# Where the words of a float64 weight are shifted and masked, in PSUM or in SBUF, in a convolution and mixing kernel on one core

## The chip, the cores and the metric

One NeuronCore of one Trainium2 chip runs the whole program. The metric is the device time of one execution in microseconds (us); lower is better. Times inside a profiled execution are counted from the start of its span.

## The reference

`x` is 8 x 4224 x 192 in float32. A softmax over seven taps weights a causal convolution along the sequence, and a low-rank mix along the sequence and a two-layer perceptron follow:

```python
w = np.exp(weight_gen - max); w = w / (sum(w) + 1e-09)       # over the 7 taps, 8 heads
out = np.einsum('bshk,bskhg->bshg', w, x_unf)                # the convolution: y
h = xt @ U @ V                                               # U: 4224 x 32, V: 32 x 4224
u = x + h.transpose(0, 2, 1)
ch = np.maximum(u @ w_ch1, 0.0) @ w_ch2                      # 192 -> 768 -> 192
return (u + ch).astype(np.float32)
```

`U`, `V`, `w_ch1` and `w_ch2` come in as float64. The kernel reads them as pairs of 32-bit words.

## The kernel before, in words

There are 88 blocks of 384 rows (11 for each of the 8 batches). A block `i` goes through the convolution (`p`: one tap's product; `acc`: their sum in PSUM; `y`), the projection `zp` of `y` on `U`, the mix `d` or `u` with `V` and the result of the projection, and the perceptron (`h`, `gh`, `gl`, `ab`, `o`). The mix needs the projection of a whole batch. So the program has a first stage, which makes the convolution of batch 0 (blocks 0 to 10) and prepares the weights, and a steady part, in which the perceptron of one block runs beside the convolution of the next batch.

**Splitting the weights.** A float64 is split into two or three fp32r parts, since TensorE multiplies in fp32r. `f64_split` (line 188) does this for a piece of up to 128 x 396 numbers, in steps that the rest of this text calls `P<part>.<step>`. There are twelve parts: 0, 1, 6 are pieces of `U`; 2, 3, 4 of `V`; 5, 8, 9 of `w_ch1`; 7, 10, 11 of `w_ch2`. Part numbers follow the loads, not quite the work: part 9 is split before part 8, and part 11 before part 10. The steps before:

- step 0, ScalarE: the high word, scaled, into the PSUM bank `pt_..._t` (Prelu with a scale);
- step 1, ScalarE: the low word into the PSUM bank `pt_..._x`;
- step 2, VectorE: the word in bank `t`, in place, shifted left by 3;
- step 3, ScalarE: bank `t` rounded to fp32r is the top part (`hi`, or straight into `ucat`, `w1h`, `w2c`);
- step 4, VectorE: bank `t` masked to its sign and exponent is `s`;
- step 5, VectorE: the low word times `s` is the low part (`lf`);
- step 6, TensorE: a matmul with minus the identity takes the top part off bank `t` (and for `w_ch1` and `w_ch2` another adds the low part);
- step 7, ScalarE: what is left in bank `t` is the rest (`r` for `V` and for part 9, otherwise straight into `ucat`, `w1l`, `w2c`).

Bank `t` is the one PSUM buffer of its pool. `hi`, `lf`, `s` and `r` are SBUF tiles of tags of their own, two buffers each.

**The three pieces of `V`.** `v_stores` (line 342) stores the parts of a piece to DRAM by three DMAs: `C<part>.0` the top, `C<part>.1` the rest (`vt<-v_r` in the profile), `C<part>.2` the low part. `v_load` (line 360) fetches a quarter of them by four DMAs into the one buffer `vq`, and `v_place` (line 368) copies that quarter into `vcat` on ScalarE. There are four such rounds, `L0 V0` to `L3 V3`; a load waits for the copy before it.

**What sets the order.** Every instruction is issued through a helper (line 30, `L30` in the profile) that keeps the program order on its engine. All DMAs are issued by SyncE, one after the other. In the first stage the order is a hand-written string, `FIRST` (line 1026), of codes: `P` steps of the split, `U` the load of a part, `C`, `L`, `V` as above, `M` products (`p` on GpSimd; `v` on VectorE, which reads the softmax weights from a copy `wq` in PSUM, code `Q`), `A` sums, `F` and `Y` first and last of a sum, `S` steps of a softmax, `x` and `D` loads of `x`, `W` loads of `weight_gen`, `Z` the projection. The line with the buffers is

```python
tiles[what] = first.tile([P, CHV], dt, tag=what, name=f"{name}_{what}", bufs=2)[:, :n]
```

Of the kernel before, what the change touches and what calls it, by code (L numbers as in the profile page):

```python
# [10 lines left out]
F32 = mybir.dt.float32  # L11
F32R = mybir.dt.float32r
I32 = mybir.dt.int32
U32 = mybir.dt.uint32
AF = mybir.ActivationFunctionType
# [29 lines left out]
def conv_moe_kernel(  # L45
# [17 lines left out]
    nc = Pinned(tc)  # L63
# [5 lines left out]
    P = 128  # L69
# [5 lines left out]
    D2 = D - P  # L75
# [106 lines left out]
    CH, CHV = 384, 396  # L182
# [5 lines left out]
    def f64_split(name, raw, n, hi, shaped, lo=None, rest=None, after=None):  # L188

        tiles = {}

        def tmp(what, dt=F32):
            if what not in tiles:
                tiles[what] = first.tile(
                    [P, CHV], dt, tag=what, name=f"{name}_{what}", bufs=2,
                )[:, :n]
            return tiles[what]  # L200

        def bank(what):
            if what not in tiles:
                pool, tag = (ps_d, "d") if what == "t" else (ps_first, "px")
                tiles[what] = pool.tile([P, 512], F32, tag=tag, name=f"pt_{name}_{what}")[:, :n]
            return tiles[what]

        low, high = raw[:, :n, 0], raw[:, :n, 1]

        def top():  # L210
            return shaped(tmp("hi", F32R)) if hi is None else hi

        def rem():
            return shaped(tmp("r")) if lo is None else lo

        def low_word():
            return rest if rest not in (None, True) else shaped(tmp("lf", F32R))

        def ti():
            return bank("t").bitcast(I32)  # L220

        def onto_t(terms):

            for m, term in terms:
                nc.tensor.matmul(
                    shaped(bank("t")), signs[m], term,
                    start=False, stop=True, skip_group_check=True,
                )


        steps = [
            lambda: nc.scalar.activation(
                bank("t"), high.bitcast(F32), AF.Prelu, scale=2.0**-112,
                alpha=-(2.0**32),
            ),
            lambda: nc.scalar.copy(bank("x"), low.bitcast(U32)),
            lambda: nc.vector.tensor_scalar(
                ti(), ti(), 3, None, op0=ALU.logical_shift_left
            ),
            lambda: nc.scalar.copy(top(), shaped(bank("t"))),  # L240
            lambda: nc.vector.tensor_scalar(
                tmp("s", I32), ti(), -(2**23), None, op0=ALU.bitwise_and
            ),
            lambda: nc.vector.scalar_tensor_tensor(
                low_word(), shaped(bank("x")), 2.0**-52,
                shaped(tmp("s", I32).bitcast(F32)), op0=ALU.mult, op1=ALU.mult,
            ),
            lambda: onto_t([(1, top())] + ([(0, low_word())] if rest is None else [])),
            lambda: nc.scalar.copy(rem(), shaped(bank("t"))),
        ]  # L250
        if after is None:
            return steps, []
        return steps, after(top, rem, low_word)
# [8 lines left out]
    def prep_u():  # L262
        n = CH // R
        src = words(u_in.rearrange("(p j) r -> p j r", p=P))
        for j0 in range(0, NJ, n):
            m = min(n, NJ - j0)
            raw = stage(f"u{j0}")
            nc.sync.dma_start(
                raw[:, : m * R].rearrange("p (j r) w -> p j (r w)", r=R),
                src[:, j0 : j0 + m],  # L270
            )
            yield f64_split(
                f"u{j0}", raw, m * R, ucat[:, j0 : j0 + m, :R],
                lambda a: a.rearrange("p (j r) -> p j r", r=R),
                ucat[:, j0 : j0 + m, R : 2 * R], ucat[:, j0 : j0 + m, 2 * R :],
            )

    def prep_w1():
        for c0 in range(0, DF, CH):
            cs = slice(c0, c0 + CH)  # L280
            ws = slice(2 * c0, 2 * (c0 + CH))
            raw = stage(f"w1a{c0}")
            nc.sync.dma_start(
                raw[:, :CH].rearrange("p n w -> p (n w)"), words(w1_in[:P])[:, ws]
            )
            yield f64_split(f"w1a{c0}", raw, CH, w1h[:, cs], flat, w1l[:, cs])

        raw = stage("w1b")
        for i in range(2):
            nc.sync.dma_start(  # L290
                raw[i * D2 : (i + 1) * D2, :CH].rearrange("p n w -> p (n w)"),
                words(w1_in[P:])[:, 2 * i * CH : 2 * (i + 1) * CH],
            )
        yield f64_split("w1b", raw, CH, None, flat, after=w1_copies)
# [684 lines left out]
    def soften(n):  # L979
# [35 lines left out]
    M1 = [0.262, -0.107, 0.14, -0.282, -0.017, -0.391]  # L1015
    M2 = [-0.081, -0.032, 1.559, 0.826, 0.748, 0.146]
# [8 lines left out]
    F_KIND = [0, 0, 1, 1, 1, 2, 0, 3, 2, 2, 3, 3]  # L1025
    FIRST = """
        I S0 x0 S0 R S0 S0 S0 S0 W1 S0 S1 U0 x1 P0.0 P0.1 M0.3p S1 P0.2 U1 S1 S1 P0.4 Q0 S1 x2
        S1 M0.2p P0.3 P0.6 U2 M0.0d P0.5 F0.2t P0.7 M0.4v P1.0 P1.2 S1 P1.4 A0.3t M1.0p P1.1
        A0.4t Q1 M0.6v M0.5v P1.3 P1.6 P1.5 A0.0t P1.7 M1.5d A0.6t Q2 P2.0 P2.2 M2.0v M1.1d W2
        M1.3v P2.3 A0.1v P2.1 F1.0t M2.2p U3 P2.4 S2 A1.2t P2.6 P2.7 Y0.5 P3.0 F2.0a A1.5t A1.1t  # L1030
        S2 M1.4v P2.5 Q3 P3.2 A2.2v D0 S2 S2 M2.5d P3.3 P3.1 x3 A1.6t P3.4 C2.1 M2.1v Z0 U4
        M2.3v M3.3p A1.3t C2.0 M3.2v P3.5 P3.6 M3.0d P3.7 U5 A1.4t P4.0 P4.2 A2.1t S2 A2.6t
        A2.3t S2 M2.4v P4.4 C2.2 Y1 P4.1 M3.4v F3.2a P4.3 A2.5t A3.3v P4.6 M3.6p S2 A3.0t Q5
        P4.7 P5.0 P4.5 M3.5v U6 M4.0d A2.4t x4 M5.0v C3.2 P5.1 P5.2 C3.1 M4.4d Z1 C3.0 W3 Q4
        M4.2v Y2 Q6 A3.1t P5.4 F4.2a P5.5 A3.6t A3.5t P5.3 P5.6 A4.0v P6.1 Z2 A4.4v S3 Y3.4
        M5.4d P5.7 P6.0 C4.1 C4.0 M4.3v F5.0a M5.2p C4.2 M5.1v M4.6v S3 A4.1t A4.3t A4.6t D1
        A5.1v P6.2 S3 A5.4v S3 P6.3 A4.5t Y4 D2 S3 M6.0v D3 P6.6 A5.2t M6.2d M5.3v P6.7 A5.5t S3
        L0 M6.5d F6.0a A6.3t S3 U7 P6.4 Z3 P6.5 M5.6v P7.0 M6.1p A6.6t P7.1 Q8 A6.2t Q7 P7.2
        P7.4 U8 A5.6v M6.4v P7.5 P7.3 V0 M8.0p P7.6 P7.7 Z4 U9 Y5.3 M7.2d P9.0 M7.0v D4 M7.5d
        A6.1t M7.1v M7.4v A6.5t P9.2 L1 A6.4t D5 F7.0a Q9 P9.1 Z5 D6 Y6 A7.4v P9.4 A7.1v F8.0a  # L1040
        M8.3v W4 M8.5d A7.2t M8.4p M8.1p M8.2v V1 P9.3 P9.5 Z6 A8.3v S4 A7.3t P9.6 A8.4v S4 Q10
        M9.0v C9.0 M9.2p M9.1p P9.7 P8.1 P8.0 A7.6v S4 M10.0p A8.1t A8.2t P8.2 P8.3 Y7.5 L2
        F9.0a U10 U11 P8.4 A8.6t M9.4v P8.5 V2 Z7 P8.6 P8.7 C9.2 A9.1t Y8.5 M9.3v M10.1d A9.2t
        P11.0 C9.1 M9.5v M10.3d S4 M9.6p A9.5t A9.3t P11.2 L3 D7 F10.0a A10.2t P11.1 P11.4 S4
        P11.5 P11.3 V3 S4 A10.1v P11.6 A9.6v A10.4v Z8 S4 Q11 T1 P11.7 A9.4t M10.5p P10.0 M10.6v
        A10.3t M11.2p A10.5t P10.2 M11.3v Y9 Y10.6 P10.3 P10.4 P10.1 D8 Z9 P10.5 M11.0d B1
        F11.2a M11.6p Z10 e0 P10.6 C9.3 d0 M11.4p D9 M11.5p A11.0v e1 A11.1v e2 d1 e3 e6 e4
        A11.3v e7 e5 A11.4t e8 D10 P10.7 D11 A11.5v Y11.6
    """
    with (  # L1050
        tc.tile_pool(name="first", bufs=2) as first,
# [165 lines left out]
```

## Time and profile before

| | |
|---|---|
| three runs | 1076.41, 1077.33, 1078.96 us; median 1077.33 us |
| the profiled execution's own time | 1078.56 us |
| its span, first to last instruction | 1076.8 us |
| TensorE matmul busy | 1062.4 us, 99% |
| VectorE, ScalarE, GpSimd busy | 912.1 us (85%), 803.1 us (75%), 843.6 us (78%) |
| mean granted TensorE clock | 0.998 of full speed |

The profiled execution took 1.23 us more than the median of the three, and 1.76 us of its time lie outside its span. Busy shares are means over two stages that differ: the first 80 us, where the weights are split, and the rest.

### The profile page before, as it was taken

What the parts mean: (1) busy time and instruction counts of PE and PEld (TensorE: products, weight loads), DVE (VectorE), ACT (ScalarE), POOL (GpSimd) and SP (SyncE); (2) the same over time, 40 slices, a digit from 0 to 9 for tenths busy, and PEclk for the clock granted to TensorE, in tenths of its full rate; (3) what the DMA queues carried; (4) which work ended last, traced back from release to release, by engine and by line L of the source; (5) the groups of instructions that cost most, each with busy time, mean ns of one, the idle gap of its engine ahead of it and who ended that gap; (6) DMA issues with size and microseconds to landing.
All of it is one profiled execution on the core that took longest, in us unless ns stands there. A gap on an engine that the chain in (4) does not pass through costs nothing.

```text
span 1076.8 us, 20185 instructions
## 1 busy us (share of the span) xinstructions
PE 1062.4 (99%) x6631; PEld 1040.8 (97%) x6631; DVE 912.1 (85%) x1704; ACT 803.1 (75%) x1934; POOL 843.6 (78%) x474
## 2 busy tenths in 40 slices
PE   7989999999999999999999999999999999999998
PEld 6768999999999999999999999999999999999998
DVE  7989899898889899898998998898998988755553
ACT  4678788877778777777777777777778777676664
POOL 8999899898988999898997999899998989400000
PEclk9999999999999999999999999999999999999999
DMA  7863444453443534444444444344443432323331
GB/s 224 238 179 98 138 120 129 119 161 102 131 134 99 156 112 123 143 118 129 133 111 130 140 116 137 111 134 135 109 144 110 118 99 83 102 75 95 90 96 48
DMA packets 132760, 133.66 MB, mean 124 GB/s; under 512 B 80696, under 2 KB 106552, under 8 KB 132528
## 3 DMA queue, kind: packets, MB, share of 16 engines
q1 hardware_dynamic: 132656, 132.38, 43.1%
q8 instruction: 52, 0.85, 0.3%
q14 instruction: 52, 0.43, 0.1%
HBM read 79.10 MB, written 53.23 MB: 123 GB/s over the span
## 4 chain that ended last, share of the span: by engine, by line
PE 92%; DMA 2%; ACT 2%; DVE 1%; POOL 1%; issue 1%; SPq 1%; ACTq 0%; POOLq 0%; DVEq 0%
PE h L30 43%; PE ab L30 42%; PE zp L30 4%; PE u L30 2%; DMA vq<-vt 1%; ACT vcat L30 1%; POOL p L30 1%; DMA w<-in_moe_w_ch_dram 1%; SPq L30 1%; DMA x<-in_x_dram 0%; DVE p L30 0%; PE d L30 0%; PE acc L30 0%; POOL wr L30 0%; PE zr L30 0%
## 5 line engine op out<-in xcount | busy, mean ns | idle before, releaser
L30 POOL TENSOR_TENSOR p<-x,wr 128x576 f32<-128x576 f32 (+1 forms) x340 | 661.3, 1965 | 70.9 <-DVE acc L30 62.6
L30 PE MATMUL ab<-w2c,gh 128*128 128x384 f32 x1584 | 482.4, 354 | 0.1
L30 ACT ACTIVATE gh<-h 128x384 fp32r<-128x384 f32 x528 | 257.5, 492 | 155.6 <-PE h L30 153.6
L30 PE MATMUL ab<-w2c,gl 128*128 128x192 f32 x1584 | 371.8, 254 | 0.0
L30 DVE SCALAR_TENSOR_TENSOR gl<-h,gh 128x384 fp32r<-128x384 f32 x528 | 282.7, 551 | 82.6 <-ACT gh L30 80.6
L30 DVE TENSOR_TENSOR acc<-acc,p 128x576 f32<-128x576 f32 x400 | 299.6, 750 | 0.4
L30 PEld LDWEIGHTS ab<-w2c,gl 128*128 128x128 f32 x1584 | 297.8, 190 | 0.0
L30 PEld LDWEIGHTS ab<-w2c,gh 128*128 128x128 f32 x1584 | 292.2, 188 | 0.6 <-ACT ab L30 0.6
L30 PE MATMUL h<-hi,w1h 128*128 128x384 f32 x528 | 182.1, 345 | 0.8 <-DVE lo L30 0.4
L30 PE MATMUL h<-lo,w1s 128*128 128x384 f32 x528 | 178.1, 337 | 0.0
L30 PE MATMUL h<-lo,w1h 128*128 128x384 f32 x528 | 177.9, 337 | 0.0
L30 PE MATMUL h<-hi,w1s 128*128 128x384 f32 x528 | 177.8, 337 | 0.0
L30 PE MATMUL h<-hi,w1l 128*128 128x384 f32 x528 | 177.7, 337 | 0.0
L30 ACT ACTIVATE ab<-u 128x384 f32<-128x384 f32 x264 | 130.0, 492 | 2.6 <-DVE o L30 2.2
L30 POOL TENSOR_TENSOR yhl<-y,yhl 128x576 fp32r<-128x576 f32 x77 | 125.3, 1628 | 5.8 <-ACT yhl L30 5.6
L30 ACT COPY o<-ab 128x192 f32<-128x192 f32 x264 | 84.8, 321 | 59.1 <-PE ab L30 51.0
L30 PEld LDWEIGHTS h<-hi,w1h 128*128 128x128 f32 x528 | 99.9, 189 | 4.3 <-DVE gl L30 2.8
L30 PEld LDWEIGHTS h<-hi,w1l 128*128 128x128 f32 x528 | 99.4, 188 | 0.0
L30 PEld LDWEIGHTS h<-lo,w1h 128*128 128x128 f32 x528 | 99.1, 188 | 0.0
L30 PEld LDWEIGHTS h<-hi,w1s 128*128 128x128 f32 x528 | 99.1, 188 | 0.0
L30 PEld LDWEIGHTS h<-lo,w1s 128*128 128x128 f32 x528 | 99.1, 188 | 0.0
L30 DVE TENSOR_TENSOR o<-ab,o 128x192 f32<-128x192 f32 x264 | 91.2, 345 | 8.9 <-ACT o L30 7.6
(120 smaller groups left out, 1204.0 us busy)
## 6 DMA issues: line engine op xcount, KB each, us to landing
turn<-sq SPq DMA_DIRECT2D x348, 72.0 KB, 1.9
out_dram<-o SPq DMA_DIRECT2D x87, 288.0 KB, 2.8
x<-in_x_dram SPq DMA_DIRECT2D x78, 288.0 KB, 3.0
uT<-turn SPq DMA_DIRECT2D x87, 192.0 KB, 2.9
uT<-turn SPq DMA_DIRECT2D x174, 96.0 KB, 2.8
wr<-in_weight_gen_dram SPq DMA_DIRECT2D x15, 336.0 KB, 3.2
x<-in_x_dram SPq DMA_DIRECT2D x8, 504.0 KB, 5.3
wr<-in_weight_gen_dram SPq DMA_DIRECT2D x9, 252.0 KB, 2.8
```

The lines of the kernel that those rows point to most:

```text
L30: return self.tc.keep_in_program_order(call(*args, **kwargs))
```

## The change

The scaled high word goes to an SBUF tile `tw` (two buffers). VectorE shifts it there in place and masks it from there, and ScalarE makes the top part from there. A new step 8, on ScalarE, copies the shifted word from `tw` into bank `t`, where TensorE takes the top part off as before. The tags `s` and `r` have one buffer instead of two.

```diff
-                    [P, CHV], dt, tag=what, name=f"{name}_{what}", bufs=2,
+                    [P, CHV], dt, tag=what, name=f"{name}_{what}",
+                    bufs=1 if what in ("s", "r") else 2,
...
+        def tw():
+            return tmp("tw")
...
         def ti():
-            return bank("t").bitcast(I32)
+            return tw().bitcast(I32)
...
             lambda: nc.scalar.activation(
-                bank("t"), high.bitcast(F32), AF.Prelu, scale=2.0**-112,
+                tw(), high.bitcast(F32), AF.Prelu, scale=2.0**-112,
                 alpha=-(2.0**32),
             ),
...
-            lambda: nc.scalar.copy(top(), shaped(bank("t"))),
+            lambda: nc.scalar.copy(top(), shaped(tw())),
...
             lambda: nc.scalar.copy(rem(), shaped(bank("t"))),
+            lambda: nc.scalar.copy(bank("t"), tw()),
         ]
...
-        S1 M0.2p P0.3 P0.6 U2 M0.0d P0.5 F0.2t P0.7 M0.4v P1.0 P1.2 S1 P1.4 A0.3t M1.0p P1.1
+        S1 M0.2p P0.3 P0.8 P0.6 U2 M0.0d P0.5 F0.2t P0.7 M0.4v P1.0 P1.2 S1 P1.4 A0.3t M1.0p
```

In `FIRST` each of the twelve parts gets its `P<part>.8` behind its step 3; nothing else in the string moves. On VectorE, TensorE, GpSimd and SyncE the instructions keep their order; ScalarE has twelve more. Three places show what moves. A name in square brackets is a semaphore that the instruction waits for; SyncE's DMAs use `DMAHW0` to `DMAHW7` in turn.

ScalarE around step 7 of part 4, the last piece of `V` (`v20`), and the start of part 5 (`w1a0`), before:

```order
L30 CAST v20_hi_363<-pt_v20_t_339 128x396 [waits DMAHW7_49,DVE_49]
L30 COPY wq_184<-wr_2_247 128x168 [waits DVE_49,Pool_49]
L30 COPY v20_r_375<-pt_v20_t_339 128x396 [waits DMAHW2_49,PE_49]
L30 ACTIVATE pt_w1a0_t_377<-w1a0_335 128x384 [waits DMAHW0_49,Activation_49]
L30 CAST pt_w1a0_x_393<-w1a0_335 128x384 [waits DVE_49]
L30 COPY wq_184<-wr_2_247 128x168 [waits DVE_49]
L30 COPY y_2_408<-acc_2_280 128x576 [waits PE_49]
```
and now:

```order
L30 CAST v20_hi_371<-v20_tw_347 128x396 [waits DMAHW7_49,DVE_49]
L30 COPY pt_v20_t_373<-v20_tw_347 128x396
L30 COPY wq_184<-wr_2_251 128x168 [waits DVE_49,Pool_49]
L30 COPY v20_r_385<-pt_v20_t_373 128x396 [waits DMAHW5_49,PE_49]
L30 ACTIVATE w1a0_tw_387<-w1a0_343 128x384 [waits DMAHW0_49]
L30 CAST pt_w1a0_x_403<-w1a0_343 128x384 [waits DVE_49]
L30 COPY wq_184<-wr_2_251 128x168 [waits DVE_49,Activation_49]
L30 COPY y_2_418<-acc_2_286 128x576 [waits PE_49]
```
The copy into bank `t` stands behind the top part, and the copy into `v20_r` waits for another DMA than before. Which one it is, SyncE's queue with the stores of the pieces of `V` tells (the order is that of before, shown of the change):

```order
L30 DMA vt2_202<-v0_lf_295 128x330 [waits DMAHW1_49,DVE_49]
L30 DMA u24_393<-in_moe_U_dram 128x576 [waits DMAHW4_49,DMAHW5_49,DMAHW3_49,DMAHW6_49,DMAHW2_49,Activation_49]
L30 DMA x_90<-in_x_dram 128x1728
L30 DMA vt2_202<-v10_lf_336 128x330 [waits DVE_49]
L30 DMA vt1_201<-v10_r_341 128x330
L30 DMA vt0_200<-v10_hi_304 128x330
L30 DMA wr_3_413<-in_weight_gen_dram 128x504 [waits DMAHW7_49,Pool_49]
L30 DMA vt1_201<-v20_r_385 128x396 [waits DMAHW0_49,Activation_49]
```
The store of `v10_r` is the 30th of SyncE's DMAs and so has `DMAHW5`. With one buffer for `r`, `v20_r` lies where `v10_r` lay, and its copy waits until that store has landed; before, it waited for the store of the first piece's `r`, which has `DMAHW2`.

ScalarE around the first copy into `vcat`, in part 7 (`w20`), before:

```order
L30 ACTIVATE pt_w20_t_512<-w20_502 128x384 [waits DMAHW2_49,DVE_49]
L30 CAST pt_w20_x_518<-w20_502 128x384 [waits DVE_49]
L30 COPY wq_184<-wr_3_403 128x168 [waits DVE_49,Pool_49]
L30 COPY wq_184<-wr_2_247 128x168 [waits Activation_49]
L30 CAST w2c_108<-pt_w20_t_512 128x2x192 [waits DVE_49]
L30 CAST vcat_104<-vq_0_490 128x33x32 [waits DMAHW6_49,DMAHW7_49,DMAHW1_49,DMAHW0_49]
L30 CAST w2c_108<-pt_w20_t_512 128x2x192 [waits PE_49]
```
and now:

```order
L30 ACTIVATE w20_tw_526<-w20_516 128x384 [waits DMAHW2_49]
L30 CAST pt_w20_x_532<-w20_516 128x384 [waits DVE_49]
L30 COPY wq_184<-wr_3_413 128x168 [waits DVE_49,Pool_49]
L30 COPY wq_184<-wr_2_251 128x168 [waits Activation_49]
L30 CAST w2c_108<-w20_tw_526 128x2x192 [waits DVE_49]
L30 COPY pt_w20_t_549<-w20_tw_526 128x384
L30 CAST vcat_104<-vq_0_504 128x33x32 [waits DMAHW6_49,DMAHW7_49,DMAHW1_49,DMAHW0_49]
L30 CAST w2c_108<-pt_w20_t_549 128x2x192 [waits PE_49,Activation_49]
```
The copy into bank `t` of part 7 now stands ahead of the first copy into `vcat`.

## Rows read from the trace of the kernel before

**Rows 1.** The table of engine time by stretch of the span (us from its start). Columns: length of the stretch, then for each engine its busy us and, in brackets, its instructions; granted TensorE clock as a share of full speed; mean busy share of the DMA engines; GB/s.

```profile
0.00:80.00 80.00, 70.54 (x293) 54.55 (x294) 67.83 (x119) 50.93 (x101) 71.34 (x54) 0.98 0.73 212
80.00:100.00 20.00, 18.61 (x106) 16.65 (x106) 17.56 (x30) 16.68 (x40) 18.63 (x11) 1.00 0.30 92
100.00:1000.00 900.00, 900.00 (x5766) 896.54 (x5764) 787.77 (x1479) 688.90 (x1681) 753.59 (x411) 1.00 0.43 121
```

**Rows 2.** The chain of work that ended last, in order of time, from 40 to 82 us. Columns: start, us, engine (SPq and the like are an engine's queue), what it wrote and the program line.

```profile
40.17 5.81 DMA w<-in_moe_w_ch_dram
...
48.18 2.15 ACT vcat L30
...
51.65 4.23 DMA vq<-vt
...
56.04 2.13 ACT vcat L30
...
59.48 3.37 DMA vq<-vt
...
62.99 2.15 ACT vcat L30
...
70.56 0.68 ACT vcat L30
...
72.56 0.31 ACT wq L30
...
75.09 0.68 DVE y L30
...
81.38 1.13 PE h L30 x5
```

**Rows 3.** Groups of VectorE's instructions in the whole span, different shapes apart. Columns: line, engine, operation, out<-in, shapes, count | busy us, mean ns of one | idle before, and what ended it.

```profile
L30 DVE TENSOR_TENSOR acc<-acc,p 128x576 f32<-128x576 f32 x400 | 299.6, 750 | 0.4
L30 DVE TENSOR_TENSOR lo<-uT,hi 64x384 fp32r<-64x384 f32 x56 | 38.9, 695 | 2.0 <-ACT hi L30 2.0
L30 DVE TENSOR_TENSOR lo<-uT,hi 128x384 fp32r<-128x384 f32 x56 | 31.4, 560 | 0.0
L30 DVE TENSOR_TENSOR lo<-d,hi 128x384 fp32r<-128x384 f32 x32 | 17.8, 555 | 8.0 <-ACT hi L30 7.7
L30 DVE TENSOR_SCALAR pt_w_t<-pt_w_t 128x384 int32<-128x384 int32 x3 | 1.7, 564 | 0.6 <-ACT pt_w_t L30 0.6
L30 DVE TENSOR_SCALAR w_s<-pt_w_t 128x384 int32<-128x384 int32 x3 | 1.7, 554 | 0.1
```

**Rows 4.** The same view for ScalarE: copies of 128x384 from SBUF to SBUF, from SBUF to PSUM and from PSUM to SBUF.

```profile
L30 ACT CAST hi<-uT 128x384 fp32r<-128x384 f32 x158 | 80.6, 510 | 0.0
L30 ACT COPY d<-uT 128x384 f32<-128x384 f32 x62 | 30.2, 487 | 0.7
L30 ACT CAST hi<-d 128x384 fp32r<-128x384 f32 x17 | 8.1, 479 | 5.9 <-PE d L30 5.4
```

**Rows 5.** ScalarE's instructions in order of time. Columns: start, us, engine, line, operation, out<-in, shape [idle before it <- what ended that idle].

```profile
30.91 0.49 ACT L30 COPY v_r<-pt_v_t 128x396 f32<-128x396 f32 x1
31.43 0.53 ACT L30 ACTIVATE pt_w1a_t<-w1a 128x384 f32<-128x384 f32 x1
46.06 0.53 ACT L30 ACTIVATE pt_w_t<-w 128x384 f32<-128x384 f32 x1 [1.46 <-DMA w<-in_moe_w_ch_dram]
47.81 0.48 ACT L30 CAST w2c<-pt_w_t 128x384 fp32r<-128x384 f32 x1 [0.23 <-DVE w_s L30]
```

**Rows 6.** The list of DMA issues in two short stretches, around the first store of `v_r` (issued at 21.33 us) and around the second (issued at 29.40 us). Columns: transfer, issuing queue, count, KB, us from issue to landing.

```profile
vt<-v_r SPq DMA_DIRECT2D x1, 165.0 KB, 1.9
...
vt<-v_r SPq DMA_DIRECT2D x1, 165.0 KB, 5.9
```

**Rows 7.** SyncE's queue in order of time; the durations are those of the issuing, not of the transfer.

```profile
29.40 0.43 SPq L30 DMA_DIRECT2D vt<-v_r  x1
34.26 2.22 SPq L30 DMA_DIRECT2D x<-in_x_dram  x3
38.42 1.70 SPq L30 DMA_DIRECT2D vq<-vt  x4
```

**Rows 8.** VectorE's instructions in order of time.

```profile
32.77 0.56 DVE L30 TENSOR_SCALAR pt_w1a_t<-pt_w1a_t 128x384 int32<-128x384 int32 x1
34.98 0.56 DVE L30 SCALAR_TENSOR_TENSOR w1a_lf<-pt_w1a_x,w1a_s 128x384 fp32r<-128x384 f32 x1 [0.53 <-DMA vt<-v_lf]
37.33 0.68 DVE L30 TENSOR_REDUCE mx<-wr 128x72 f32<-128x504 f32 x1 [0.25 <-DMA wr<-in_weight_gen_dram]
46.62 0.57 DVE L30 TENSOR_SCALAR pt_w_t<-pt_w_t 128x384 int32<-128x384 int32 x1 [0.37 <-ACT pt_w_t L30]
```

**Rows 9.** TensorE's instructions in order of time: the first words matmul.

```profile
11.09 0.47 PE L30 MATMUL pt_u_t<-ucat,sign 128*128 128x384 f32 x1 [2.49 <-ACT ucat L30]
```

**Rows 10.** The table by stretch again, two shorter stretches.

```profile
11.00:15.00 4.00, 3.91 (x9) 2.86 (x10) 3.41 (x7) 2.25 (x6) 3.92 (x4) 0.57 0.67 169
20.00:30.00 10.00, 9.77 (x43) 7.81 (x43) 10.00 (x18) 6.21 (x14) 8.75 (x6) 1.00 0.61 156
```

**Rows 11.** VectorE's instructions in order of time in the steady part: one with both inputs in SBUF.

```profile
224.85 0.68 DVE L30 TENSOR_TENSOR lo<-uT,hi 128x384 fp32r<-128x384 f32 x1
```

**Rows 12.** GpSimd's instructions in order of time around it.

```profile
219.55 8.07 POOL L30 TENSOR_TENSOR p<-x,wr 128x1152 f32<-128x1152 f32 x4
```

More of the change, by code (lines that the diff above doesn't have):

```diff
@@ L1027, in conv_moe_kernel @@
         I S0 x0 S0 R S0 S0 S0 S0 W1 S0 S1 U0 x1 P0.0 P0.1 M0.3p S1 P0.2 U1 S1 S1 P0.4 Q0 S1 x2
-        S1 M0.2p P0.3 P0.6 U2 M0.0d P0.5 F0.2t P0.7 M0.4v P1.0 P1.2 S1 P1.4 A0.3t M1.0p P1.1
[L1029 to L1048, printed above, removed]
+        S1 M0.2p P0.3 P0.8 P0.6 U2 M0.0d P0.5 F0.2t P0.7 M0.4v P1.0 P1.2 S1 P1.4 A0.3t M1.0p
+        P1.1 A0.4t Q1 M0.6v M0.5v P1.3 P1.8 P1.6 P1.5 A0.0t P1.7 M1.5d A0.6t Q2 P2.0 P2.2 M2.0v
@@ new lines, in conv_moe_kernel @@
+        M1.1d W2 M1.3v P2.3 P2.8 A0.1v P2.1 F1.0t M2.2p U3 P2.4 S2 A1.2t P2.6 P2.7 Y0.5 P3.0
+        F2.0a A1.5t A1.1t S2 M1.4v P2.5 Q3 P3.2 A2.2v D0 S2 S2 M2.5d P3.3 P3.8 P3.1 x3 A1.6t
+        P3.4 C2.1 M2.1v Z0 U4 M2.3v M3.3p A1.3t C2.0 M3.2v P3.5 P3.6 M3.0d P3.7 U5 A1.4t P4.0
+        P4.2 A2.1t S2 A2.6t A2.3t S2 M2.4v P4.4 C2.2 Y1 P4.1 M3.4v F3.2a P4.3 P4.8 A2.5t A3.3v
+        P4.6 M3.6p S2 A3.0t Q5 P4.7 P5.0 P4.5 M3.5v U6 M4.0d A2.4t x4 M5.0v C3.2 P5.1 P5.2 C3.1
+        M4.4d Z1 C3.0 W3 Q4 M4.2v Y2 Q6 A3.1t P5.4 F4.2a P5.5 A3.6t A3.5t P5.3 P5.8 P5.6 A4.0v
@@ new lines, in conv_moe_kernel @@
+        P6.1 Z2 A4.4v S3 Y3.4 M5.4d P5.7 P6.0 C4.1 C4.0 M4.3v F5.0a M5.2p C4.2 M5.1v M4.6v S3
+        A4.1t A4.3t A4.6t D1 A5.1v P6.2 S3 A5.4v S3 P6.3 P6.8 A4.5t Y4 D2 S3 M6.0v D3 P6.6 A5.2t
+        M6.2d M5.3v P6.7 A5.5t S3 L0 M6.5d F6.0a A6.3t S3 U7 P6.4 Z3 P6.5 M5.6v P7.0 M6.1p A6.6t
+        P7.1 Q8 A6.2t Q7 P7.2 P7.4 U8 A5.6v M6.4v P7.5 P7.3 P7.8 V0 M8.0p P7.6 P7.7 Z4 U9 Y5.3
+        M7.2d P9.0 M7.0v D4 M7.5d A6.1t M7.1v M7.4v A6.5t P9.2 L1 A6.4t D5 F7.0a Q9 P9.1 Z5 D6
+        Y6 A7.4v P9.4 A7.1v F8.0a M8.3v W4 M8.5d A7.2t M8.4p M8.1p M8.2v V1 P9.3 P9.8 P9.5 Z6
@@ new lines, in conv_moe_kernel @@
+        A8.3v S4 A7.3t P9.6 A8.4v S4 Q10 M9.0v C9.0 M9.2p M9.1p P9.7 P8.1 P8.0 A7.6v S4 M10.0p
+        A8.1t A8.2t P8.2 P8.3 P8.8 Y7.5 L2 F9.0a U10 U11 P8.4 A8.6t M9.4v P8.5 V2 Z7 P8.6 P8.7
+        C9.2 A9.1t Y8.5 M9.3v M10.1d A9.2t P11.0 C9.1 M9.5v M10.3d S4 M9.6p A9.5t A9.3t P11.2 L3
+        D7 F10.0a A10.2t P11.1 P11.4 S4 P11.5 P11.3 P11.8 V3 S4 A10.1v P11.6 A9.6v A10.4v Z8 S4
+        Q11 T1 P11.7 A9.4t M10.5p P10.0 M10.6v A10.3t M11.2p A10.5t P10.2 M11.3v Y9 Y10.6 P10.3
+        P10.8 P10.4 P10.1 D8 Z9 P10.5 M11.0d B1 F11.2a M11.6p Z10 e0 P10.6 C9.3 d0 M11.4p D9
@@ L1049, in conv_moe_kernel @@
+        M11.5p A11.0v e1 A11.1v e2 d1 e3 e6 e4 A11.3v e7 e5 A11.4t e8 D10 P10.7 D11 A11.5v Y11.6
     """
```

## The prediction, made before the run

> **What bounds the kernel now.** I read the engine time by stretch first. From 100 to 1000 us TensorE is busy 900.00 of 900 us, so a microsecond that the first stage loses or gains reaches the end whole, and nothing in the steady part, where the change has no instruction, can give it back [rows 1]. In the first 80 us no engine is alone the bound: GpSimd 71.34, TensorE 70.54, VectorE 67.83, ScalarE 50.93 us busy [rows 1]. All twelve splits lie there. The second view was the chain of waits through that stage. It waits for a piece of `w_ch2` (DMA at 40.17, 5.81 us), runs through that piece's words on ScalarE and VectorE to the first copy into `vcat` at 48.18, and then through the four rounds of load and copy of `V` (48.18, 56.04, 62.99, 70.56), which leave no gap: each load is issued when the copy before it ends, and each copy starts when the load has landed. Behind the fourth come a `wq` copy, the last sums of `y`, and the first `h` at 81.38 [rows 2]. So the sum is: how much later or earlier does the first copy into `vcat` start, what do the four rounds and the tail add, and all of it goes on top of the time.
>
> **VectorE's 24 shifts and masks.** Before, 564 and 554 ns each at 384 columns [rows 3]. No row shows an instruction with one SBUF input and an SBUF output of this shape, so I bound it. Nearest above: `lo<-uT,hi`, whose tiles all lie in SBUF, 560 ns at the same shape, against 555 with one input in PSUM: no gain [rows 3]. Below: `acc` at 576 columns and `lo` at 384 differ by 195 ns over 192 columns, 1.02 ns a column; if SBUF let two columns through at a time, 192 columns' worth, 0.20 us, would go. I take 0.10 us, halfway, since neither end has a row of its own. Over 24 that is 2.4 us of VectorE time, 0 to 4.8.
>
> [...]
>
> **ScalarE's twelve new copies.** SBUF to PSUM at 384 columns takes 487 ns (`d<-uT`); reading the top part from SBUF instead of PSUM costs 510 against 479 ns; writing the scaled word to SBUF likewise some 30 ns [rows 4]. Together 12 x (0.49 + 0.03 + 0.03) = 6.6 us of ScalarE time, nearly all beside other work, since ScalarE is idle 29 of the first 80 us [rows 1]. On the path lies only part 7's copy, directly ahead of the first copy into `vcat`: +0.42 us, start to start. Against it, ScalarE's top part no longer waits for VectorE's mask of the same bank, which cost 0.23 us of idle in part 7 [rows 5]; it can start right behind the shift. If the idle time went, each new copy would add its 0.42 us.
>
> **The one buffer for `r`.** Here is the new wait. Step 7 of part 4 (`v_r`, 30.91 us [rows 5]) now waits until the store of part 3's `r` has landed. That store is issued at 29.40; a store like it landed after 1.9 us when the queue was short, and this one took 5.9 us [rows 6, 7]. So the copy starts at 35.3 (by the shorter row at 31.3). I take 35.3: the store stands behind a large load of `x`, and nothing ahead of it in SyncE's queue changes. ScalarE stops 4.4 us.
>
> Behind it on ScalarE stands step 0 of part 5, before at 31.43, 0.53 us long [rows 5]; it now ends at 36.35. VectorE's shift of part 5, before at 32.77, waits for that, so VectorE, after two products, stands still and starts it at 36.4: 3.6 us late. Until the shift of part 7 (46.62) VectorE gets back its own old waits, 0.53 + 0.25 + 0.37 = 1.15 us [rows 8], and 4 x 0.10 on the four shifts and masks between. It is 2.05 us late there. ScalarE, TensorE and GpSimd wait behind VectorE's products and sums for the same while; none of them is later than that.
>
> **The DMAs.** The three stores of part 4 are issued 4.4 us later, the three loads of `x` behind them (2.22 us of issuing) too, so the first `vq` load, before at 38.42, cannot be issued ahead of some 39.6, and the piece of `w_ch2` goes out at 41.4 instead of 40.17 [rows 2, 7]. By 5.81 us of flight it lands at 47.2 at the latest. ScalarE's step 0 of part 7, which waited 1.46 us for it [rows 5], is wanted by VectorE at 48.7; so the DMAs are late inside VectorE's lag and add nothing.
>
> **To the first copy into `vcat`.** Before, it started 1.56 us after the shift of part 7. Now: shift 0.47, top part 0.42, new copy 0.42, 1.35 us with handovers. So it is 2.05 - 0.2 = 1.85 us late, at 50.0. The four rounds carry this on unchanged: what the new copies of parts 9, 8 and 11 add falls into the time in which those loads fly. In the tail VectorE's shift of part 10 stands ahead of the last `y` and saves 0.10. Sum: 1.85 - 0.10 = **+1.75 us**. The profiled execution would take 1078.56 + 1.75 = 1080.3; it stands 1.23 us above the median of the runs shown, so I forecast 1077.33 + 1.75 = **1079.1 us**. With 0 to 0.20 us for the words and half a microsecond on the landing, this case spans 1077.9 to 1080.5.
>
> **Rivals.**
>
> *The wait is given back.* If the store lands early, with fewer writes behind it (31.3 to 33.5 instead of 35.3), VectorE's lag at part 7 is 0 to 0.3 us, and what is left is that lag, the 0.2 us less from shift to `vcat` copy and the 0.10 of the tail: 1076.9 to 1077.5, taken as 1077.3. For it: DMA flight here ranges from 1.9 to 5.9 us. Against: the load ahead of the store is not changed.
>
> *Faster.* VectorE is busy 10.00 of 10 us from 20 to 30 us [rows 10], and four of the words stand there. If each gives 0.20 us, SyncE's load behind part 4's low word and all stores go out 0.8 us earlier; if in addition the landing is early as above, `w_ch2` is issued 0.8 us earlier. With 0.2 us less at part 7, 0.2 for its faster shift, 0.2 in the tail, and a load of the second round that no longer takes 4.23 us but the 3.37 of the third [rows 2], 2.3 us go: 1075.0. It decides at a landing before 31.3 and words under 0.40 us. Against it: the chain's rounds wait for DMAs, not for VectorE.
>
> [...]
>
> *VectorE and GpSimd block each other.* In the steady part a VectorE instruction with both inputs in SBUF took 0.68 us in the middle of GpSimd products [rows 11, 12], against 560 ns in the mean: 0.12 us more. At 24 words 2.9 us of VectorE time, which would eat the saving and leave 1080 to 1081, within the other cases. If a word had to wait for a whole product to end (8.07 us for four, so 1.0 us on average), VectorE would lose 24 us where it has 12 idle: +8 to +12 us, 1087. For it speaks that GpSimd works 89% of the stage; against it, that the row shows 0.12 us and not 1.0.
>
> [...]
>
> **How the numbers follow.** About 0.2% (2.15 us) can be told from no change by a measurement of this kernel. Chances: forecast 0.50, given back 0.18, clock and whole wait 0.20, blocking 0.06, faster 0.06. Slower by over 0.2% is above 1079.5: of the forecast's case 0.16, the clock's 0.20, blocking 0.06, together 0.42. Faster is 0.06; 0.52 stays within. The range leaves out faster (0.06), blocking (0.06) and the far ends of the cases beside them (0.06): 1076.6 to 1082.5. All but 0.06 lies on one side of a small step, so the likeliest case's own range is 1077.9 to 1080.5.
>
> **What would show it.** In the changed profile: `v_r` of part 4 on ScalarE some 4 us later, with DMA `vt<-v_r` as what ended its wait; an idle VectorE of 3 to 4 us ahead of the shift of part 5; the first `vcat` copy near 50.0, the fourth near 72.4, the first `h` near 83.1; shifts and masks between 0.36 and 0.56 us; twelve copies of 0.49 us. Wrong would be: `v_r` without a wait for a DMA; the shift of part 7 at or before 46.6; words over 0.7 us or GpSimd products that grow; a half-speed stretch of TensorE's clock behind 37 us.

## The result, and the profile after

The changed kernel takes **1091.26 us** (median of four runs, 1089.87 to 1094.56) against 1076.87 (four runs, 1076.30 to 1078.96): a ratio of 1.0134, 95% interval 1.0107 to 1.0162. Forecast were 1079.1 us and a range up to 1082.5, so the change costs some 14 us where 1.75 were foreseen. The profiled execution took 1089.87 us, its span 1088.0. That is 11.2 us more than the span before. The execution profiled before (1078.56 us) lay above its median and this one is the shortest of its four, so the traces account for 11.2 of the 14.4 us between the medians.

Read the stretches first. Engine busy time by stretch, in the changed kernel:

```profile
0.00:80.00 80.00, 64.51 (x247) 48.98 (x248) 67.80 (x103) 47.05 (x97) 62.83 (x46) 0.94 0.64 191
100.00:1000.00 900.00, 899.65 (x5757) 895.59 (x5757) 790.95 (x1483) 690.90 (x1685) 763.86 (x416) 1.00 0.43 121
```

The columns are those of [rows 1]: TensorE, its weight loads, VectorE, ScalarE, GpSimd, then clock, DMA share and GB/s. The steady part is as full as before. In the first 80 us TensorE did 64.51 us of work instead of 70.54 and GpSimd 62.83 instead of 71.34, while VectorE was as busy as before, with less done. Next the chain of waits through that stage:

```profile
25.12 2.21 DVE v_tw L30
...
28.76 2.01 DVE v_s L30
...
35.06 5.96 DMA vt<-v_r
...
41.49 0.57 ACT w1a_tw L30
42.08 1.80 DVE w1a_tw L30
...
56.48 1.16 DVE w_tw L30
...
66.43 2.12 ACT vcat L30
...
71.47 1.36 DVE w1a_tw L30
...
78.63 1.25 DVE w_s L30
...
92.64 1.12 PE h L30 x5
```

Before, this chain was loads and copies of `V` [rows 2]; now it runs mostly through VectorE, through its words and, in lines left out here, its products and sums, with one landing of `v_r` between them. The first `h` starts at 92.64 instead of 81.38: 11.26 us, the 11.2 by which the span grew. The words by form (the columns are those of [rows 3]):

```profile
L30 DVE TENSOR_SCALAR u_s<-u_tw 128x384 int32<-128x384 int32 x2 | 3.6, 1818 | 0.0
L30 DVE TENSOR_SCALAR w_s<-w_tw 128x384 int32<-128x384 int32 x3 | 3.5, 1170 | 0.1
L30 DVE TENSOR_SCALAR v_tw<-v_tw 128x330 int32<-128x330 int32 x2 | 3.3, 1637 | 1.6 <-ACT v_tw L30 1.6
L30 DVE TENSOR_SCALAR w1a_tw<-w1a_tw 128x384 int32<-128x384 int32 x2 | 3.2, 1583 | 4.1 <-ACT w1a_tw L30 4.1
...
L30 DVE TENSOR_SCALAR w1b_tw<-w1b_tw 128x384 int32<-128x384 int32 x1 | 0.3, 346 | 0.0
L30 DVE TENSOR_SCALAR w1b_s<-w1b_tw 128x384 int32<-128x384 int32 x1 | 0.3, 343 | 0.0
```

One shape, 384 columns, takes 0.34 us in one place and 1.8 in another, where it took 0.55 to 0.57 everywhere before [rows 3]. All 24 together, over all forms of this view, take 23.8 us instead of 12.9. What the long ones wait for is not in the idle column: the wait lies inside the instruction's own time. It shows when two engines are laid beside each other. GpSimd in order of time, in two stretches:

```profile
24.93 2.22 POOL L30 TENSOR_TENSOR p<-x,wr 128x1152 f32<-128x1152 f32 x1
...
28.36 2.21 POOL L30 TENSOR_TENSOR p<-x,wr 128x1152 f32<-128x1152 f32 x1
```

and VectorE over the same time:

```profile
22.39 0.32 DVE L30 TENSOR_SCALAR v_s<-v_tw 128x330 int32<-128x330 int32 x1
...
25.12 2.21 DVE L30 TENSOR_SCALAR v_tw<-v_tw 128x330 int32<-128x330 int32 x1
...
28.68 2.08 DVE L30 TENSOR_SCALAR v_s<-v_tw 128x330 int32<-128x330 int32 x1
```

The products end at 27.15 and 30.57, the two words at 27.33 and 30.76: 0.18 and 0.19 us behind them, whenever they began. The word at 22.39 met an idle GpSimd (it was waiting until 23.60) and took 0.32 us. Of all 24 words 20 met a running GpSimd instruction and end 0.17 to 0.23 us behind it; three met an idle GpSimd. So a word with both ends in SBUF waits until the running GpSimd instruction is over. The 24th word shows that GpSimd can lose too:

```profile
64.20 2.44 POOL L30 TENSOR_TENSOR p<-x,wr 128x1152 f32<-128x1152 f32 x1 [1.03 <-PE acc L30]
```

```profile
64.22 0.34 DVE L30 TENSOR_SCALAR w1b_s<-w1b_tw 128x384 int32<-128x384 int32 x1
```

The two begin within 0.02 us; here the word takes its 0.34 us and the product 2.44 instead of 2.22. A product behind a waiting word starts 0.14 to 0.26 us before the word ends and takes, where it is a double one, 2.33 to 2.35 us, some 0.1 more, so the mean of the double products grew from 2226 to 2259 ns in the first 95 us: GpSimd loses little, VectorE much.

The other foreseen loss is there too. ScalarE around the second `v_r`, which answers to [rows 5]:

```profile
41.10 0.49 ACT L30 COPY v_r<-pt_v_t 128x396 f32<-128x396 f32 x1 [4.27 <-DMA vt<-v_r]
41.49 0.56 ACT L30 ACTIVATE w1a_tw<-w1a 128x384 f32<-128x384 f32 x1
...
58.49 2.12 ACT L30 CAST vcat<-vq 128x1056 fp32r<-128x1056 f32 x1
...
80.86 2.12 ACT L30 CAST vcat<-vq 128x1056 fp32r<-128x1056 f32 x1 [0.33 <-DMA vq<-vt]
```

Start against start with the kernel before, the lag grows in steps: 2.3 us at `v_tw` of part 3 (25.12 against 22.78), 5.7 at part 4's shift, 9.31 at part 5's (42.08 against 32.77 [rows 8]), 9.78 at part 7's (56.40 against 46.62 [rows 8]), 10.3 at the first `vcat` copy, 11.26 at the first `h`. The two blocked words of 2.21 and 2.08 us make 3.3 of it, the wait of `v_r` 3.6; the rest are other words and, in the first 25 us, probably also TensorE's clock, below.

### The profile page after: what moved, and what is told of

Read it like the earlier page. It is cut to its first block, busy times and chain, and to the rows that moved or that the text cites. A ratio compares the mean times of both kernels' runs of the same rounds, so it can differ in the third digit from the quotient of the medians.

```text
span 1088.0 us, 20194 instructions
## 1 busy us (share of the span) xinstructions
PE 1066.5 (98%) x6631; PEld 1042.6 (96%) x6631; DVE 922.8 (85%) x1704; ACT 807.8 (74%) x1946; POOL 845.4 (78%) x474
## 4 chain that ended last, share of the span: by engine, by line
PE 92%; DVE 4%; DMA 1%; ACT 1%; issue 1%; SPq 0%; ACTq 0%; DVEq 0%
PE h L30 43%; PE ab L30 42%; PE zp L30 4%; PE u L30 2%; DVE p L30 1%; PE acc L30 1%; DVE acc L30 1%; DMA vt<-v_r 1%; DMA u<-in_moe_U_dram 1%; DVE sm L30 0%; PE d L30 0%; DVE w1a_tw L30 0%; DVE y L30 0%; PE zr L30 0%; DVE v_tw L30 0%
```

## Experiments

Theory A: a word with both ends in SBUF waits for the running GpSimd product. Theory B: the one buffer of `r`. Theory C: the twelve ScalarE copies. Every kernel below is the changed one or the one before with one thing altered; but wherever `tw` is kept and `r` has two buffers, `tw` has one instead of two, so that the space is the same. What that alone costs was not measured. Times in us over the kernel before are (ratio - 1) x 1078; the expectations, written earlier, quote differences of medians instead (8.35 and 2.93 for the first two). Words are all 24 shifts and masks of the profiled execution.

| kernel | SBUF words | r buffers | median us | ratio (95%) | us over before | words: sum, longest us |
|---|---|---|---|---|---|---|
| words, no wait | 24 | 2 | 1086.38 | 1.0069 (1.0054 to 1.0084) | +7.4 | 21.0, 2.20 |
| wait only | 0 | 1 | 1080.96 | 1.0024 (1.0013 to 1.0035) | +2.6 | 12.8, 0.57 |
| shift into the bank | 0 | 2 | 1077.34 | 0.9992 (0.9983 to 1.0001) | -0.9 | 12.8, 0.57 |
| two inputs | 24 | 2 | 1091.64 | 1.0127 (1.0110 to 1.0144) | +13.7 | 28.6, 2.49 |
| changed, again | 24 | 1 | 1091.53 | 1.0123 (1.0105 to 1.0142) | +13.3 | 23.9, 2.21 |
| masks only | 12 | 2 | 1080.65 | 1.0021 (1.0010 to 1.0031) | +2.3 | 19.2, 2.23 |
| copies alone | 0 | 2 | 1079.01 | 1.0007 (0.9997 to 1.0017) | +0.8 | 12.9, 0.57 |
| copies and wait | 0 | 1 | 1082.15 | 1.0038 (1.0027 to 1.0049) | +4.1 | 12.9, 0.57 |
| V words only | 6 | 2 | 1082.79 | 1.0045 (1.0030 to 1.0060) | +4.9 | 17.8, 2.21 |
| all but V words | 18 | 2 | 1082.15 | 1.0034 (1.0022 to 1.0046) | +3.7 | 18.5, 1.79 |
| words, half products | 24 | 2 | 1084.24 | 1.0050 (1.0034 to 1.0067) | +5.4 | 21.6, 1.28 |
| before, half products | 0 | 2 | 1078.45 | 1.0001 (0.9992 to 1.0010) | +0.1 | 12.9, 0.57 |

**Words without the wait.**

```diff
-                    bufs=1 if what in ("s", "r") else 2,
+                    bufs=1 if what in ("s", "tw") else 2,
```

> The changed kernel, but the remainder r has two buffers again (s and tw one each, so the space is the same): the words stay in SBUF and the twelve ScalarE copies stay, the wait of v_r for its store to DRAM goes. Theory A (each one-input word in SBUF waits for the end of the GpSimd product that runs): the words' 10.8 us more of VectorE time stay, so about 1086 to 1090, with words of up to 2.3 us in the trace. Theory B (the one buffer of r costs it: 5.96 us of landing on the chain): about 1077 to 1079. Theory C (the twelve copies, 6.6 us of ScalarE): as A, but with words of 0.4 us and ScalarE as the releaser on the chain.

+7.4 us (5.8 to 9.1), words of up to 2.20 us. More than half of the loss has nothing to do with the buffers of `r`. The copies, which are still in this kernel, are left to a later run.

**The wait alone.** The kernel before with

```diff
-                    [P, CHV], dt, tag=what, name=f"{name}_{what}", bufs=2,
+                    [P, CHV], dt, tag=what, name=f"{name}_{what}",
+                    bufs=1 if what == "r" else 2,
```

> The kernel before with one buffer for r and nothing else: the wait alone. Theory A, with the forecast's own working of the wait: 1077.0 + 1.75 = 1078.6 (1077 to 1080), v_r 4.3 us late. Theory B: 1085 to 1091, most of the 14 us. Theory C: as A.

+2.6 us (1.4 to 3.8), a little over the 1077 to 1080 expected. ScalarE shows the wait itself as forecast:

```profile
37.30 0.49 ACT L30 COPY v_r<-pt_v_t 128x396 f32<-128x396 f32 x1 [4.67 <-DMA vt<-v_r]
```

The forecast's 1.75 lies inside the interval. So does 3.45, an estimate for the wait with one more slow stretch of TensorE's clock on top, like that of the kernel before, 0.57 from 11 to 15 us [rows 10]: 1.75 and 0.43 x 4 = 1.7 us. The ten runs fall into two groups: six with a mean granted clock of 0.993 to 0.995 took 1080.76 to 1084.18 us, four with 0.997 to 1.00 took 1078.54 to 1079.65. Against the 1078.03 us before, their medians are about 3.3 and 1.1 us longer. So both cases seem to occur; the run profiled is of the first group, and its clock is 0.83 from 40 to 50 us.

**Shift into the bank.** The scaled word goes to SBUF as in the change, but the shift writes bank `t`, mask and top part read the bank, and there is no step 8.

```diff
-                ti(), ti(), 3, None, op0=ALU.logical_shift_left
+                bank("t").bitcast(I32), ti(), 3, None, op0=ALU.logical_shift_left
...
-                tmp("s", I32), ti(), -(2**23), None, op0=ALU.bitwise_and
+                tmp("s", I32), bank("t").bitcast(I32), -(2**23), None,
+                op0=ALU.bitwise_and,
```

> ScalarE still writes the scaled word to SBUF, but VectorE's shift reads it there and writes the PSUM bank, the mask reads the bank, and step 8 is gone; r has two buffers. No word has both ends in SBUF, no wait, no copies. Theories A, B and C all say about 1077 (1075.5 to 1078.5); it shows whether anything else of the change (Prelu into SBUF) costs. Words of 0.45 to 0.6 us.

-0.9 us (-1.8 to 0.1): no loss, and no gain that can be told. Its trace has the control for the two blocked words. GpSimd, then VectorE:

```profile
20.71 2.22 POOL L30 TENSOR_TENSOR p<-x,wr 128x1152 f32<-128x1152 f32 x1
```

```profile
20.74 0.49 DVE L30 TENSOR_SCALAR pt_v_t<-v_tw 128x330 int32<-128x330 int32 x1
```

The same shift begins 0.03 us behind the start of a 2.22 us product and takes 0.49 us. With one end in the bank it doesn't wait.

**Two inputs.** As the first, but each word reads a second SBUF operand, the shift a column of ones and the mask the word itself:

```diff
-            lambda: nc.vector.tensor_scalar(
-                tmp("s", I32), ti(), -(2**23), None, op0=ALU.bitwise_and
+            lambda: nc.vector.scalar_tensor_tensor(
+                tmp("s", I32), ti(), -(2**23), ti(),
+                op0=ALU.bitwise_and, op1=ALU.bitwise_and,
```

> [...] Theory A: nothing waits for GpSimd; words of 0.5 to 0.7 us each, and about 1077 to 1079. Theory C (copies): 1084 to 1090, as in the first. Theory B: 1077 to 1079 as in the first. So a gap between this and the first is the waiting of one-input words alone.

A clear miss: +13.7 us, the worst of all. I expected no waiting with two inputs, by [rows 11, 12] once more. The trace, GpSimd and then VectorE:

```profile
25.09 2.22 POOL L30 TENSOR_TENSOR p<-x,wr 128x1152 f32<-128x1152 f32 x1
```

```profile
22.38 0.49 DVE L30 SCALAR_TENSOR_TENSOR v_s<-v_tw 128x330 int32<-128x330 int32 x1
...
25.29 2.38 DVE L30 SCALAR_TENSOR_TENSOR v_tw<-v_tw,ones 128x330 int32<-128x330 int32 x1
```

The product ends at 27.31, the word at 27.67. A word with two SBUF inputs waits just as long, and then runs longer: 0.49 us alone at 330 columns instead of 0.32. The kernel before has such waits too. GpSimd and VectorE there, around 227 us:

```profile
225.08 2.54 POOL L30 TENSOR_TENSOR p<-x,wr 128x1152 f32<-128x1152 f32 x1
```

```profile
227.31 0.72 DVE L30 TENSOR_TENSOR lo<-uT,hi 64x384 fp32r<-64x384 f32 x1
```

The product ends at 227.62 and `lo` at 228.03, 0.41 us behind it. It had been waiting all along. Of the 56 `lo` of this shape 48 met a running product; they took 0.71 to 0.73 us and end 0.41 or 0.42 us behind it. The other eight met an idle GpSimd and took 0.55 us. So the mean of 695 ns in [rows 3], longer than the 560 ns at twice the partitions, was itself this wait; it looked small because the product had only 0.3 us to go. The instruction of [rows 11] is the same. The product that it met was

```profile
223.91 1.20 POOL L30 TENSOR_TENSOR p<-x,wr 128x576 f32<-128x576 f32 x1
```

It ends at 225.11, and the instruction of [rows 11] at 225.53, 0.42 us behind. The product of 225.08 above starts while that instruction runs, and takes 2.54 us instead of 2.22.

**The parts on one chip.** First the changed kernel again, unaltered.

> The changed kernel once more, beside the next three on one chip, so that the parts can be added up. So far: words alone +8.35 us, wait alone +2.93, together 11.3; the changed kernel stood 14.4 above the kernel before. If the parts add, about 1089 (ratio 1.0095 to 1.011); if wait and words make each other worse, 1091 again (1.0125 or more).

+13.3 us (11.3 to 15.3).

**Masks only.** The scaled word goes to bank `t`, and only the shift's result to SBUF:

```diff
-                tw(), high.bitcast(F32), AF.Prelu, scale=2.0**-112,
+                bank("t"), high.bitcast(F32), AF.Prelu, scale=2.0**-112,
...
-                ti(), ti(), 3, None, op0=ALU.logical_shift_left
+                ti(), bank("t").bitcast(I32), 3, None, op0=ALU.logical_shift_left
```

> As the words without the wait (r with two buffers, twelve copies), but the scaled word is written to the PSUM bank and the shift reads it there and writes SBUF: of the 24 words only the 12 masks have both ends in SBUF. Theory A (a word with both ends in SBUF waits for the GpSimd product that runs): shifts of 0.45 to 0.57 us, masks still of up to 2.3; about half of the 8.35 us, so 1081 to 1083.5. If the loss came from the copies, or from the scaled word in SBUF: 1085 to 1088 or 1077.

+2.3 us (1.1 to 3.3), in the range named, but less than half of 7.4. The shifts, now with their source in the bank, take 0.45 to 0.56 us; the masks lose 6.5 us of VectorE time in all. Most of it cost nothing:

```profile
24.70 0.38 DVE L30 TENSOR_SCALAR v_s<-v_tw 128x330 int32<-128x330 int32 x1
...
33.88 1.74 DVE L30 TENSOR_SCALAR w1a_s<-w1a_tw 128x384 int32<-128x384 int32 x1
```

The mask that took 2.08 us in the changed kernel came 0.2 us before the end of a product here and took 0.38. And the 1.74 us one lies ahead of waits that VectorE had before (0.53 and 0.25 us [rows 8]): the shift of the next part starts only 0.3 us later than before, at 41.58 against 41.25.

**Copies alone, copies and wait.** The kernel before with a step 8 that copies bank `t` to a tile that nobody reads, and `r` with two buffers or one:

```diff
+            lambda: nc.scalar.copy(tw(), bank("t")),
```

> The kernel before plus one ScalarE copy a part at the place of the new one, from the PSUM bank to an SBUF tile that nobody reads: twelve copies of 0.48 us that the words matmul has to wait for, no word in SBUF, r with two buffers. Theory A: +0 to +1 us, 1077 to 1079. Theory C (the copies cost it): 1081 to 1085.

> The twelve copies of the run before this one, and one buffer for r: everything of the change but the words in SBUF. Theory A: as the wait alone, +2 to +4 us, 1079.5 to 1082. If wait and copies pile up on ScalarE: 1083 to 1086.

+0.8 us (-0.3 to 1.8) and +4.1 (2.9 to 5.3). Theory C falls, as far as copies from the bank to SBUF stand for the change's own, which go the other way. The parts add to 7.4 + 4.1 - 0.8 = 10.7 of 13.3 us, each with one or two microseconds of uncertainty. Whether the rest is the wait and the words making each other worse, `tw`'s second buffer, or more time at the lower clock (0.992 to 0.994 in the mean of the changed kernel's runs here, 0.995 in those of the words without the wait) is open.

**Where the words cost.** The next two put SBUF words into the three parts of `V` alone, or into the nine others alone; the other parts keep their words in the bank and the unread copy.

```diff
+        sb = name[0] == "v"
...
-            return tw().bitcast(I32)
+            return (tw() if sb else bank("t")).bitcast(I32)
```

> SBUF words in the three parts of V alone (6 of the 24), in the other nine parts the words stay in the PSUM bank with the unread copy of ScalarE, r has two buffers. Theory A with phase (a word costs what is left of the GpSimd product it meets, and counts whole where VectorE has no idle time): in the run with all words in SBUF and no wait, two words of the second V part took 2.20 and 2.09 us, 3.3 us more than before, where VectorE is busy 10.00 of 10 us. With 0.8 us for the copies: +3.5 to +4.5, 1081.5 to 1083. If all words cost alike (7.4 us over 24): +1.8 and 0.8, 1080.5 to 1081.3.

> The opposite: SBUF words in the nine parts that are not V's (18 of the 24). Theory A with phase: what the first of this pair leaves of 7.4 us and the copies: +3.5 to +5, 1081.5 to 1083.5. If all words cost alike: +5.6 and 0.8, 1084.5 to 1085.5.

+4.9 us (3.2 to 6.5) and +3.7 (2.4 to 5.0); less the copies counted twice, 7.8 against 7.4 for all. By the medians six words of 24 cost as much as the other 18 or more, though the intervals overlap. Two of the six took 2.21 and 2.09 us at 23.14 and 26.70 us, where VectorE has no idle time.

**Half the product.** The double products of the first stage as two instructions, in the kernel with SBUF words and in the kernel before:

```diff
+        for i in range(2):
+            nc.gpsimd.tensor_tensor(
+                pk[:, i].rearrange("p t (h g) -> p t h g", h=H),
...
```

> All 24 words in SBUF, r with two buffers, and each double product of GpSimd in the first stage (1152 elements, 2.2 us) issued as two of 576 (1.2 us). Theory A (a word waits for the end of the running GpSimd instruction): no word over 1.5 us, and 3 to 6 us above the next run. If the loss has nothing to do with GpSimd's instructions: words of up to 2.2 us still, and 7 to 8 us above the next run.

> The kernel before with the same halved products, for comparison: GpSimd gets some 18 x 0.23 = 4 us more work in a stage where it is busy 89%, so +1 to +4 us, 1079 to 1082; words of 0.57 us.

5.3 us apart, and no word over 1.28 us. Halving alone costs nothing that can be told (+0.1 us, -0.9 to 1.1), where I had expected +1 to +4. The two words of part 3:

```profile
23.01 1.19 DVE L30 TENSOR_SCALAR v_tw<-v_tw 128x330 int32<-128x330 int32 x1
...
25.55 1.06 DVE L30 TENSOR_SCALAR v_s<-v_tw 128x330 int32<-128x330 int32 x1
```

2.21 and 2.08 us became 1.19 and 1.06: the longest waits are as long as GpSimd's instruction, a product of 1.23 us in the mean here. The sum over all words did not fall (21.6 us), because more of them met a running GpSimd instruction: 23 of 24 end 0.16 to 0.25 us behind one, against 18 of 24 with whole products. The 5.3 us alone would not settle it, since their uncertainty of 2 us reaches the 7.4; the lengths of the words do.

## Why the prediction was wrong

*The failed step: "VectorE and GpSimd block each other", and with it the sum's term for the 24 shifts and masks.* The sum had each word 0.10 us shorter; for the blocking I took 0.12 us a word from [rows 11, 12], and against the case that a word waits for a whole product I said that "the row shows 0.12 us and not 1.0". The row could not show 1.0: it met a product with 0.26 us to go, and the four products were lumped as 8.07 us x4, so that I did not see where one ended. Measured: up to 2.39 us a word, 23.8 us instead of 12.9 for all 24 in the changed kernel.

The rival's price, 1087 us with "+8 to +12", came near the words without the wait (1086.38, +7.4), but partly by luck: it counted 24 us of VectorE time, where the words lost 8.1 us in that run and 10.9 in the changed kernel. Its chance of 0.06 and the range that left it out were wrong. What sizes the loss is how much of a product is left when a word comes, and whether VectorE has idle time behind it.

Two inputs did not keep a word from waiting, though I had read the 0.68 us of [rows 11] so: words of both kinds end 0.18 to 0.36 us behind a 2.2 us product in the rows above, and `lo` ended 0.41 us behind one before.

*What bounds the kernel: right.* The steady part gave nothing back; the first `h` was 11.26 us late and the span 11.2 longer.

*The words by themselves: right in kind, too small.* I took 0.10 us a word, between 0 and 0.20. A 384-column word takes 0.34 to 0.35 us when GpSimd is idle, 0.2 us less than before, so the far end was the right one. That saving is worth nothing beside waits of 1 to 2 us.

*ScalarE's copies: right.* 474 ns each against 490 taken, and +0.8 us (-0.3 to 1.8) for all twelve, made the other way round.

*The one buffer for `r`: right in mechanism, near in size.* `v_r` waited 4.27 us for the store (forecast 4.4), and part 5's shift fell back by 9.31 - 5.67 = 3.64 us (forecast 3.6). Alone it costs 2.6 us (1.4 to 3.8) against 1.75. In the changed kernel the return of 1.5 us by part 7 did not come (9.31 us late at part 5, 9.78 at part 7): there the shift of part 5 took 1.80 us.

*The four rounds: as long as forecast, by luck.* 58.49 to 80.86 is 22.37 us, as before from 48.18 to 70.56 [rows 2]. But the copies no longer wait for loads (the last waits 0.33 us); the chain between them runs through VectorE's words (71.47, 78.63).

*The DMAs: right.* Step 0 of part 7 starts at 54.38 and waits for no load; that of the second piece of `w_ch2` was issued at 46.24.

*Clock and whole wait, the case with the chance of 0.20: seen, sized only in part.* From 11 to 15 us the granted clock was 0.50, against 0.57 before [rows 10]; it was still 0.72 from 15 to 20 us, and from 30 to 40 it was 0.83, with 0.50 in every half microsecond from 31.5 to 34.5 and 1.00 from 35 on:

```profile
11.00:15.00 4.00, 3.31 (x7) 2.50 (x8) 3.96 (x6) 2.52 (x7) 3.11 (x3) 0.50 0.51 147
20.00:30.00 10.00, 8.49 (x37) 6.29 (x35) 10.00 (x13) 6.19 (x15) 7.94 (x6) 1.00 0.40 106
30.00:40.00 10.00, 8.52 (x30) 6.65 (x31) 8.41 (x14) 2.52 (x6) 6.64 (x5) 0.83 0.67 203
```

The granted clock is the third number from the end. Ahead of that half-speed stretch, from 20 to 30 us, TensorE had been busy 8.49 of 10 us. Words without the wait show 0.83 from 30 to 40 us too; the wait alone shows 1.00 there and 0.83 from 40 to 50, behind the late `v_r`. So a slow stretch came with either loss; what sets it off was not shown. The upper end of the range, 1082.5, rested on the price of such a stretch, which no run shows by itself; for the wait alone the two groups of runs (3.3 and 1.1 us over before) put it at some 2 us, an estimate from their medians. The words cost without it, too. In the profiled run of V words only the clock behind 20 us stays at full speed:

```profile
30.00:90.00 60.00, 54.60 (x250) 42.81 (x248) 55.68 (x91) 45.29 (x89) 54.64 (x35) 1.00 0.65 190
```

and its first `h` still starts at 84.95, 3.6 us late; the two longest words there alone are 3.3 us longer than before. What the clock adds to the 7.4 us of all words was not separated.

## What to carry to other kernels

Before both ends of a VectorE instruction go into SBUF, look at GpSimd: price the instruction at what is left of the GpSimd instruction it will meet, up to that one's whole length (a word took up to 2.39 us beside a double product of 2.22), and keep one end in PSUM where that is not wanted (0.49 us beside such a product). When a row is to show whether two engines disturb each other, compare where their instructions end, one by one; a small excess may only mean that little was left to wait for, and a row that lumps four hides it. Lay those that met the other engine at work beside those that met it idle: 0.72 and 0.55 us stood in the kernel before. An added wait costs in full only where its engine has no idle time behind it: the masks of one kernel lost 6.5 us of VectorE time and cost 2.3.

## What the runs showed of the hardware

Not expected: a VectorE word with two SBUF inputs waited for GpSimd like one with one input (2.38 us beside a 2.22 us product). For a word with one input, one end in the PSUM bank was enough to avoid it, whichever end: 0.49 us with the output there, 0.45 to 0.56 with the input there, beside running products. The wait stands as busy time of VectorE (2.21 us for the word at 25.12), neither as idle time nor with a releaser. And where the word got in first, GpSimd waited: 2.44 us for a product of 2.22 beside a word of 0.34.
